# Retention and routed experts on one core: value products between the turns, casts and differences apart, decays by half, a head two products ahead

## The chip, the cores and the metric

The kernel runs on one core of a Trainium2 chip. Its time is the device time in microseconds, taken as the median of three runs. TensorE is called PE in the rows, VectorE DVE, ScalarE ACT, GpSimd POOL and SyncE SP.

## What is computed

Per batch and head a state of 64 x 64 decays and collects k v; each token's output is its query times the state. All 3072 tokens then go through a mixture of 8 experts: each token to the expert with the highest logit, weighted by that expert's probability and by a sigmoid.

```python
for t in range(S):                                   # B, H, S, D = 4, 8, 768, 64
    state = gamma * state + einsum('bhd,bhe->bhde', k[:, :, t], v[:, :, t])
    y[:, :, t] = scale * einsum('bhd,bhde->bhe', q[:, :, t], state)
x = y.transpose(0, 2, 1, 3).reshape(B * S, H * D)    # 3072 x 512
e_idx = argmax(x @ w_gate); probs = softmax(x @ w_gate); eom = sigmoid(x @ w_output_gate)
for e in range(8):                                   # w1[e]: 512 x 1024, w2[e]: 1024 x 512
    out[mask_e] = probs[mask_e, e] * eom[mask_e, e] * (relu(x[mask_e] @ w1[e]) @ w2[e])
```

## The kernel before

It has three parts. **Attention and routing** run over 12 pairs of chunks of 128 tokens (three pairs a batch). For a pair j, `load_pair` (L216) brings k, q and v on SyncE's queue, two pairs ahead; `prep_q` and `prep_v` (L255, L249) copy q and multiply v with its decays on GpSimd; `turn_k` and `turn_q` (L282, L291) transpose on TensorE, and ScalarE copies the results out of PSUM. `scores` (L302) multiplies keys and queries, and VectorE masks the result into `am` (L310). `inter` (L315) adds the part carried in the state, `attend(j, c)` (L325) the masked scores times v, one call for each chunk c; `weigh(j, c)` (L332) multiplies with the query decays on VectorE, and `state(j, c)` (L338) updates the state. Routing of pair j - 1 runs inside pair j: `logits`, `turn_l`, `route1`, `exps`, `tokens`, `counts`, `labels`, `places`, `gates`, `rows` (L350 to L462). `scatter(j, c)` (L472) writes the rows of a chunk, sorted by expert, to HBM with an indirect DMA of GpSimd. The order on every engine is the order of the calls (L594 to L750): nothing is rescheduled.

**The head** is the first 256 rows of the expert that has most tokens after pair 2 (`pick`). After pair 8 its count is checked (`late`, L678 and L679), all engines read that flag in pair 10 (L620), and the rows are loaded (`head_load`, L518) and prepared (`head_prep`, L527). Products run as a generator (`head_all`, L573), 192 steps of one product, advanced by `run_head(n)`: block f of the first layer (`head_stage1`, 12 products, a relu on ScalarE and the remainder of it on VectorE, L553 and L554), then block f - 1 of the second (`head_stage2`, 12 products). It fills TensorE while the last pair is routed.

**The expert loop** (L901) goes over the rest of that expert and the seven others in order of their counts, eight blocks each. Each float32 operand is split in a rounded part (a cast on ScalarE) and a difference (VectorE), and three products make one. `load_weights(s)` (L137) loads block s, and `split_weights(s)` (L148) makes both parts: two casts (L158, L159), two differences (L160, L161); `w_at` says which blocks are loaded in which pair. `load_x` (L760) loads an expert's sorted rows, `prep_x` (L777) transposes and splits them. `load_x(0)` waits for all scatters and for the `pad` of unused slots; the pads for the other experts (`new_pad`, L875) and the SyncE reads of the seven ranks (L712) come before it or around it.

Buffers matter where they make waits: two wide PSUM tiles `w` (each of scores, turns and tokens takes the next), one PSUM tile each for y0, y1, state and `misc`, three buffers `raw` (weights, the head's rows and at first the decays), two for v, three for k, one for the copied q.

Of the kernel before, what the change touches and what calls it, by code (L numbers as in the profile page):

```python
# [10 lines left out]
F32 = mybir.dt.float32  # L11
# [21 lines left out]
def retention_moe_kernel(  # L33
# [101 lines left out]
    raws, wts, rank_e = {}, {}, {}  # L135
# [12 lines left out]
    def split_weights(s: int):  # L148
# [11 lines left out]
        nc.vector.tensor_sub(lo[:, 0], raw[:, 0], hi[:, 0].bitcast(F32))  # L160
        nc.vector.tensor_sub(perm(lo), r2, perm(hi).bitcast(F32))  # L161
        wts[s] = (hi, lo)

# [26 lines left out]
    with tc.manual_schedule(engines=None), ExitStack() as actx:  # L190
# [25 lines left out]
        def load_pair(j):  # L216
            load2(kn, k, "kn", j, 3)
            load_q(j)
            load2(vn, v, "vn", j, 2)
# [6 lines left out]

        load2(kn, k, "kn", 0, 3)
        nc.gpsimd.memset(wg, 0.0)
        nc.scalar.dma_start(gv, dec_v)
        nc.scalar.dma_start(wg[:, 0, :, 0:E], w_gate.rearrange("(g p) e -> p g e", p=P))  # L230
        nc.scalar.dma_start(wg[:, 0, :, E:2 * E], w_ogate.rearrange("(g p) e -> p g e", p=P))
        load_q(0)
        load2(vn, v, "vn", 0, 2)
        nc.sync.dma_start(gqn[:, 0].rearrange("p g t -> p (g t)"), dec_q.unsqueeze(1).broadcast_to([2, D, NG * P]))
        nc.sync.dma_start(gc[:, 0].rearrange("p c g -> p (c g)"), dec_c.unsqueeze(1).broadcast_to([2, D, NC * NG]))
        load_pair(1)

        def swap_halves():
            for n, h in enumerate(half):
                nc.gpsimd.tensor_copy(wg[h, 1, :, 0:2 * E], wg[half[1 - n], 0, :, 0:2 * E])  # L240
            for n, h in enumerate(half):
                nc.gpsimd.tensor_copy(gc[h, 1], gc[half[1 - n], 0])
                nc.gpsimd.tensor_copy(gqn[h, 1], gqn[half[1 - n], 0])
# [5 lines left out]
        def prep_v(j, engine):  # L249
            c = 2 * (j % NJ)  # L250
            vs[j] = ap.tile([P, 2, H, D], F32, name="vs", tag="vs", bufs=2)
            engine.tensor_mul(vs[j].rearrange("p c h d -> p (c h) d"), vn.pop(j).rearrange("p c h d -> p (c h) d"),
                              gv[:, c:c + 2].rearrange("p c h -> p (c h)").unsqueeze(2).broadcast_to([P, 2 * H, D]))
# [10 lines left out]
        prep_v(0, nc.gpsimd)  # L264
# [4 lines left out]
        pw = ps_1.tile([P, 512], F32, name="pw", tag="y1")  # L269
# [20 lines left out]

        def turn_q(j, halved=False):  # L291
# [10 lines left out]
        def scores(j):  # L302
            for c in range(2):
                w = wide()
# [9 lines left out]

        def inter(j):  # L315
            rt["py"] = [ps_1.tile([P, 512], F32, name="py", tag=f"y{c}") for c in range(2)]
# [8 lines left out]
        def attend(j, c):  # L325
            py = rt["py"][c]
            for g in range(NG):
                for hh in range(2):
                    nc.tensor.matmul(py[half[hh ^ c], g * P:(g + 1) * P], vs[j][:, c, 2 * g + hh], ams[c][:, hh, g],
                                     start=(j % NJ == 0 and c == 0 and g == 0), stop=True, skip_group_check=True)  # L330

# [18 lines left out]
        def logits(j):  # L350
            misc = rt["misc"] = ps_1.tile([P, 512], F32, name="misc", tag="misc")
# [17 lines left out]
        def route1(j):  # L369
# [3 lines left out]
            m2b = m2.unsqueeze(2).broadcast_to([P, 2, E])  # L373
            key = sm.tile([P, 2, E], F32, name="key2", tag="key2")
# [7 lines left out]
            d16 = sm.tile([P, 2, E], F32, name="d16", tag="d16")  # L382
            nc.vector.tensor_tensor(out=d16, in0=lg[:, :, 0:E], in1=m2b, op=ALU.subtract)
# [25 lines left out]
        def counts(j):  # L409
# [11 lines left out]
            for c in range(2):  # L421
                nc.gpsimd.tensor_add(acc, acc, oh[:, c])
# [49 lines left out]
        def scatter(j, c):  # L472
# [4 lines left out]
            tc.declare_no_dep(st.ins, group="srt", reason="rows are disjoint")  # L477
            tc.add_to_no_dep_group("srt", st.ins)
            sent.append(st.ins)
# [18 lines left out]
        def sort8(c8, last, by):  # L498
# [15 lines left out]
        w_at = {4: (0,), 5: (1,), 6: (2,), 7: (3,), 8: (4,), 9: (5,), 10: (6, 7)}  # L514
# [3 lines left out]
        def head_load():  # L518
            t = wpool.tile([P, 8 * SEG], F32, name="xl0", tag="raw", bufs=3).rearrange("p (n x) -> p n x", x=SEG)
            for a in range(4):  # L520
# [3 lines left out]
                behind(ld, sent)  # L524
            hd["t"] = t

        def head_prep():  # L527
            t = hd["t"]
            hd["xh"] = hpool.tile([P, NDC, HEAD], F32R, name="xh0")
            hd["xl"] = hpool.tile([P, NDC, HEAD], F32R, name="xw0")  # L530
            for g in range(2):
# [5 lines left out]
                nc.vector.tensor_sub(hd["xl"][:, 2 * g:2 * g + 2], tp, hd["xh"][:, 2 * g:2 * g + 2].bitcast(F32))  # L537
            hd["idx"] = hpool.tile([P, HEAD // 32], I32, name="idx0")
            nc.vector.tensor_copy(hd["idx"], t[:, :, P])

        def head_stage1(f):
            hi, lo = wts[f]
            ps = ps_1.tile([P, 512], F32, name="h0", tag="st" if f == 0 else f"y{1 - f % 2}")[:, 0:HEAD]
            n = 0
            for r, ls in (("xh", (hi, lo)), ("xl", (hi,))):
                for dc in range(NDC):
                    for l in ls:
                        nc.tensor.matmul(ps, l[:, 0, dc * P:dc * P + P], hd[r][:, dc], start=(n == 0), stop=(n == 3 * NDC - 1))
                        n += 1
                        if n < 3 * NDC:  # L550
                            yield
# [41 lines left out]

        idle(9)  # L594
# [464 lines left out]
```

## Time and profile before

| | us |
|---|---|
| median of three runs (459.74 to 460.03) | 459.8 |
| the profiled execution | 461.23 |
| its span, first to last instruction | 459.5 |
| TensorE busy in the span | 422.1 |
| VectorE, ScalarE, GpSimd busy | 268.6, 177.8, 187.3 |

The profiled execution is 1.43 us above the median; 1.73 us of it lie outside its span. A busy TensorE need not be one at its best, since products are pipelined and their ends are modelled: the starts of neighbouring products tell the pace. Idle time is shown in brackets with what ended it.

### The profile page before, as it was taken

The page shows a single profiled execution, that of the slowest core. Times are in us where ns is not written, and L with a number is a line of the kernel's source. Part 1 is how long each engine was busy: PE and PEld are TensorE (multiplying, and loading weights), DVE is VectorE, ACT ScalarE, POOL GpSimd, SP SyncE. Part 2 cuts the span into 40 slices and gives each one's busy share as a digit, 9 for nine tenths or more (in the row PEclk, how much of TensorE's full clock was granted, in tenths as well). Part 3 has the DMA queues.
Part 4 walks back from the last instruction along what each step waited for, and adds up shares of the span by engine and source line. Part 5 has one row for each costly group of instructions (what it writes and reads, how often), then busy time and mean ns, then how long its engine had stood idle before and what let it go on. Part 6 is the DMA issues. An engine that isn't in the chain of part 4 may idle for free.

```text
span 459.5 us, 10306 instructions
## 1 busy us (share of the span) xinstructions
PE 422.1 (92%) x3701; PEld 401.6 (87%) x3701; DVE 268.6 (58%) x703; ACT 177.8 (39%) x392; POOL 187.3 (41%) x255
## 2 busy tenths in 40 slices
PE   8689999999696986999999999999999999999991
PEld 4579998888585986999999999999999999999990
DVE  2567777877866644684655656565565566565110
ACT  2034544555352511463443443444344353443111
POOL 5245666665611420643102442452452452441532
PEclk9979999999987997999999999999999999999997
DMA  8798689999631239469438448547547648630102
GB/s 151 178 233 195 173 227 264 278 272 268 191 84 35 95 83 228 152 219 247 132 106 196 149 142 184 169 143 181 167 162 166 185 157 184 199 121 14 36 18 69
DMA packets 126818, 74.15 MB, mean 161 GB/s; under 512 B 56854, under 2 KB 115098, under 8 KB 126756
## 3 DMA queue, kind: packets, MB, share of 16 engines
q1 hardware_dynamic: 119828, 59.57, 51.7%
q0 software_dynamic: 5728, 13.76, 8.4%
q8 instruction: 31, 0.51, 0.5%
q14 instruction: 31, 0.25, 0.2%
q10 hardware_dynamic: 1200, 0.06, 0.2%
HBM read 59.62 MB, written 15.23 MB: 163 GB/s over the span
## 4 chain that ended last, share of the span: by engine, by line
PE 51%; issue 7%; POOL 3%; DVE 1%; DMA 1%; ACT 0%; POOLq 0%; ACTq 0%
PE h L803 26%; PE a L821 24%; POOL out_dram L165 3%; DMA srt<-zrow,padr 1%; PE w L569 1%; DVE xt L789 0%; ACT xh L790 0%; DVE xw L791 0%; POOL srt L175 0%; POOLq L165 0%; ACT h L553 0%; POOLq L933 0%; DVE padr L738 0%; DVE ordf L730 0%; DVE ck L733 0%
## 5 line engine op out<-in xcount | busy, mean ns | idle before, releaser
L165 POOL DMA_INDIRECT out_dram<-ot,idi x83 | 86.9, 1047 | 151.2 <-ACT hh L807 123.8
L803 PE MATMUL h<-xh,whi 128*128 128x192 f32 (+7 forms) x256 | 86.6, 338 | 0.0
L803 PE MATMUL h<-xh,wlo 128*128 128x192 f32 (+7 forms) x256 | 86.5, 338 | 0.0
L803 PE MATMUL h<-xw,whi 128*128 128x192 f32 (+7 forms) x256 | 86.5, 338 | 0.0
L821 PE MATMUL a<-hl,whi 128*128 128x192 f32 (+7 forms) x256 | 85.7, 335 | 0.0
L821 PE MATMUL a<-hh,wlo 128*128 128x192 f32 (+7 forms) x256 | 85.7, 335 | 0.0
L821 PE MATMUL a<-hh,whi 128*128 128x192 f32 (+7 forms) x256 | 85.6, 335 | 0.0
L808 DVE SCALAR_TENSOR_TENSOR hl<-h,hh 128x192 fp32r<-128x192 f32 (+7 forms) x64 | 34.8, 544 | 66.9 <-ACT hh L807 66.7
L160 DVE TENSOR_TENSOR wlo<-raw,whi 128x512 fp32r<-128x512 f32 x64 | 44.2, 690 | 36.8 <-ACT whi L158 36.8
L807 ACT ACTIVATE hh<-h 128x192 fp32r<-128x192 f32 (+7 forms) x64 | 30.7, 480 | 88.8 <-PE h L803 88.8
L158 ACT CAST whi<-raw 128x512 fp32r<-128x512 f32 x64 | 39.8, 622 | 37.7 <-PE a L821 34.6
L803 PEld LDWEIGHTS h<-xh,whi 128*128 128x128 f32 x256 | 49.1, 192 | 0.5
L803 PEld LDWEIGHTS h<-xw,whi 128*128 128x128 f32 x256 | 49.0, 191 | 0.5
L803 PEld LDWEIGHTS h<-xh,wlo 128*128 128x128 f32 x256 | 48.9, 191 | 0.5
L821 PEld LDWEIGHTS a<-hl,whi 128*128 128x128 f32 x256 | 48.2, 188 | 0.6
L821 PEld LDWEIGHTS a<-hh,whi 128*128 128x128 f32 x256 | 48.2, 188 | 0.5
L821 PEld LDWEIGHTS a<-hh,wlo 128*128 128x128 f32 x256 | 48.3, 189 | 0.4
L161 DVE TENSOR_TENSOR wlo<-raw,whi 128x512 fp32r<-128x512 f32 x64 | 45.4, 709 | 0.0
L159 ACT CAST whi<-raw 128x512 fp32r<-128x512 f32 x64 | 39.7, 620 | 0.0
L474 POOL DMA_INDIRECT srt<-row,posi x24 | 24.6, 1026 | 17.8 <-ACT row L460 13.2
L790 ACT CAST xh<-xt 128x416 fp32r<-128x416 f32 (+3 forms) x32 | 16.3, 510 | 40.1 <-DVE xt L789 35.9
L310 DVE TENSOR_TENSOR am<-w,mask 128x1024 f32<-128x1024 f32 x24 | 28.3, 1215 | 5.5 <-PE w L307 5.5
(170 smaller groups left out, 633.3 us busy)
## 6 DMA issues: line engine op xcount, KB each, us to landing
raw<-in_moe_w_dram SPq DMA_DIRECT2D x128, 256.0 KB, 3.0
kn<-in_k_dram SPq DMA_DIRECT2D x24, 256.0 KB, 5.7
qn<-in_q_dram SPq DMA_DIRECT2D x12, 512.0 KB, 6.8
vn<-in_v_dram SPq DMA_DIRECT2D x24, 256.0 KB, 6.0
xl<-srt SPq DMA_DIRECT2D x12, 211.2 KB, 5.6
xl<-srt SPq DMA_DIRECT2D x12, 195.0 KB, 5.3
out_dram<-ot,idi POOLq DMA_INDIRECT x83, 2.6
xl<-srt SPq DMA_DIRECT2D x4, 227.5 KB, 6.5
```

The source lines that it names most:

```text
L158: nc.scalar.copy(hi[:, 0], raw[:, 0])
L159: nc.scalar.copy(perm(hi), r2)
L160: nc.vector.tensor_sub(lo[:, 0], raw[:, 0], hi[:, 0].bitcast(F32))
L161: nc.vector.tensor_sub(perm(lo), r2, perm(hi).bitcast(F32))
L165: st = nc.gpsimd.indirect_dma_start(out=dst, out_offset=bass.IndirectOffsetOnAxis(ap=idx, axis=0), in_=src, in_offset=None, bounds_check=n ...
L310: nc.vector.tensor_tensor(out=a.rearrange("p b g t -> p (b g) t"), in0=w.rearrange("p b (g t) -> p (b g) t", g=NG), in1=mask.rearrange("p ...
L474: st = nc.gpsimd.indirect_dma_start(out=srt, out_offset=bass.IndirectOffsetOnAxis(ap=posi[:, c:c + 1], axis=0), in_=row[:, c].rearrange("p ...
L790: nc.scalar.copy(xh[:, dc, w], tp[:, w])
L803: nc.tensor.matmul(ps[:, 0:C], l[:, 0, w], r[:, dc, 0:C], start=(n == 0), stop=(n == 3 * NDC - 1))
L807: relu = nc.scalar.activation(hh, ps[:, 0:C], AF.Relu)
L808: nc.vector.scalar_tensor_tensor(out=hl, in0=ps[:, 0:C], scalar=0.0, in1=hh.bitcast(F32), op0=ALU.max, op1=ALU.subtract)
L821: mm = nc.tensor.matmul(accs[d][:, 0:C], l[:, 1, w], r, start=(f == 0 and n == 0), stop=(f == NF - 1 and n == 2))
```

## The change

It rewrites the order of calls in pairs and tail, and some helpers. In the start, q is loaded first, k and v behind it; the decays of the queries come as two DMAs of 64 rows each in place of one DMA of [2, 64, 512], likewise the chunk decays; the gate weights are loaded later; `prep_v` of pairs 0 and 1 works in two halves; pair 0 is written out apart, with the state of pair 1 inside its scores. From pair 2 on k is loaded behind q and v. In a pair, GpSimd prepares the next q and v ahead of its first scatter; `attend(j, 0)` and `weigh(j, 0)` stand between the turns of k and q; the second scatter waits for that `attend`. `split_weights` becomes `cast_weights` (right behind the scores) and `low_weights` (behind the first weighing). Weights are loaded in pairs 4, 6, 8 and 9 only. The padding of the head's expert and the check of its count come in pairs 9 and 10. The head runs its first-layer blocks two ahead of the second layer, in three PSUM tiles. The SyncE reads of the seven ranks and the small operations behind them come after `load_x(0)`; nine operations that make the last flag come after the head.

```diff
@@ loads at the start
+        load_q(0)
         load2(kn, k, "kn", 0, 3)
+        load2(vn, v, "vn", 0, 2)
...
-        nc.sync.dma_start(gqn[:, 0].rearrange("p g t -> p (g t)"), dec_q.unsqueeze(1).broadcast_to([2, D, NG * P]))
+        for n, h in enumerate(half):
+            nc.sync.dma_start(gqn[h, 0].rearrange("p g t -> p (g t)"), dec_q[n:n + 1].broadcast_to([D, NG * P]))
@@ weights
+    def cast_weights(s: int):
...
         nc.scalar.copy(hi[:, 0], raw[:, 0])
         nc.scalar.copy(perm(hi), r2)
-        nc.vector.tensor_sub(lo[:, 0], raw[:, 0], hi[:, 0].bitcast(F32))
-        nc.vector.tensor_sub(perm(lo), r2, perm(hi).bitcast(F32))
         wts[s] = (hi, lo)
+        def rest():
+            nc.vector.tensor_sub(lo[:, 0], raw[:, 0], hi[:, 0].bitcast(F32))
+            nc.vector.tensor_sub(perm(lo), r2, perm(hi).bitcast(F32))
+        subs[s] = rest
@@ head
-            for f in range(1, NF):
+            yield from head_stage1(1)
+            for f in range(2, NF):
                 yield from head_stage1(f)
-                yield from head_stage2(f - 1)
+                yield from head_stage2(f - 2)
+            yield from head_stage2(NF - 2)
             yield from head_stage2(NF - 1)
@@ pairs, the new order
+        for j in range(1, NPR - 1):
             if j + 2 < NPR:
                 load_pair(j + 2)
...
+            prep_q(j + 1, nc.gpsimd)
+            prep_v(j + 1, nc.gpsimd)
+            if j >= 2 and j - 2 != EARLY:
+                scatter(j - 2, 0)
+            open_y()
+            scores(j, (lambda: state(1, 0)) if j == 1 else None)
+            if j - 1 in w_at:
+                cast_weights(w_at[j - 1])
             inter(j)
...
+            logits(j - 1)
+            turn_k(j + 1)
+            turn_l(j - 1)
+            route1(j - 1)
+            exps(j - 1)
+            done = attend(j, 0)
+            weigh(j, 0)
+            turn_q(j + 1)
+            gates(j - 1)
             if j >= 2 and j - 2 != EARLY:
-                scatter(j - 2, 1)
+                scatter(j - 2, 1, [done])
...
+            if j - 1 in w_at:
+                low_weights(w_at[j - 1])
             if j % NJ < NJ - 1:
                 state(j, 1)
+            tokens(j - 1)
+            labels(j - 1)
+            rows(j - 1)
+            counts(j - 1)
+            places(j - 1)
...
+            if j - 1 == EARLY:
+                judge()
             attend(j, 1)
             weigh(j, 1)
+            state(j + 1, 0)
@@ between head and loop
         load_x(0)
+        io_ = mp.tile([P, E], F32, name="io_", bufs=1)
...
+        for r in range(1, E):
+            rank_e[r] = nc.values_load(order[0:1, r - 1:r], engines=(mybir.EngineType.SP,), min_val=0, max_val=E - 1)
...
+        cast_weights(7)
+        low_weights(7)
         run_head(24)
         new_pad(hd["relu", 6])
+        run_head(12)
+        turn_x(0, 0)
+        turn_x(0, 1)
+        low_x(0, 0)
...
+        run_head(12)
+        new_pad(hd["relu", 7])
         run_head(1000)
```

## Rows read from the trace of the kernel before

**Rows 1.** From the page's second part: the clock granted to TensorE in 40 equal slices of the span, in tenths.

```profile
PEclk9979999999987997999999999999999999999997
```

**Rows 2.** Busy time of each engine by stage; columns: stretch and its length, busy time (instructions) of PE, PE's weight loads, DVE, ACT, POOL, granted clock, DMA share, GB/s. The cuts are the first score products of pairs 0, 1, 3, 4, 5, 6, 10, 11, then pair 11 and the head to the loop.

```profile
10.45:26.12 15.67, 9.73 (x144) 8.22 (x144) 9.02 (x12) 2.42 (x5) 5.99 (x8) 0.91 0.76 183
26.12:37.75 11.63, 11.45 (x174) 10.52 (x172) 6.30 (x28) 4.27 (x12) 4.02 (x8) 0.83 0.93 182
47.05:56.98 9.93, 9.75 (x163) 8.89 (x159) 6.86 (x30) 5.12 (x15) 6.38 (x11) 1.00 0.68 176
56.98:66.75 9.77, 9.59 (x177) 8.75 (x173) 7.66 (x35) 4.77 (x14) 6.00 (x10) 1.00 0.85 215
66.75:75.98 9.23, 9.10 (x159) 8.27 (x156) 6.15 (x28) 3.91 (x12) 5.59 (x10) 1.00 0.92 256
75.98:118.30 42.32, 39.12 (x647) 34.67 (x643) 33.05 (x119) 23.27 (x61) 27.69 (x41) 1.00 1.04 268
118.30:133.32 15.02, 11.05 (x176) 10.26 (x173) 11.20 (x33) 5.78 (x16) 5.95 (x10) 0.89 0.45 135
133.32:143.10 9.78, 5.43 (x93) 4.87 (x90) 6.73 (x12) 3.22 (x8) 1.03 (x1) 0.81 0.26 83
143.10:150.75 7.65, 6.63 (x62) 6.14 (x61) 4.40 (x26) 2.39 (x9) 2.65 (x7) 0.80 0.09 35
150.75:173.30 22.55, 21.04 (x188) 20.44 (x187) 12.38 (x67) 6.42 (x19) 7.43 (x12) 1.00 0.30 93
173.30:180.48 7.18, 3.06 (x14) 2.81 (x14) 2.90 (x9) 1.69 (x5) 0.98 (x1) 0.75 1.12 224
```

**Rows 3.** The timeline of the start: start and length in us, engine, line, operation, out<-in, shape, count, and in brackets the idle time before it with what ended it.

```profile
10.21 1.90 POOL L252 TENSOR_TENSOR vs<-vn,gv 128x1024 f32<-128x1024 f32 x1 [3.92 <-DMA vn<-in_v_dram]
...
18.95 0.66 PE L286 MATMUL w<-ident,kn 128*128 128x128 f32 x4 [1.21 <-DMA kn<-in_k_dram]
...
23.11 1.90 POOL L252 TENSOR_TENSOR vs<-vn,gv 128x1024 f32<-128x1024 f32 x1 [5.39 <-DMA vn<-in_v_dram]
...
25.07 1.12 PE L344 MATMUL st<-vs,kn 128*64 128x64 f32 x16 [2.52 <-POOL vs L252]
```

**Rows 4.** Stretches of the start, columns as in rows 2: ahead of, during and behind the load of the decays.

```profile
4.50:7.00 2.50, 2.50 (x13) 1.76 (x12) 0.00 (x0) 0.00 (x0) 1.53 (x15) 1.00 1.24 241
...
10.50:12.00 1.50, 1.50 (x24) 1.50 (x26) 0.15 (x1) 0.46 (x1) 1.50 (x1) 1.00 0.13 49
...
15.75:18.00 2.25, 2.00 (x38) 1.59 (x34) 1.40 (x2) 0.37 (x1) 1.93 (x4) 1.00 1.04 260
```

**Rows 5.** The timeline of pair 6, columns as in rows 3: the second weight difference and the turn of k.

```profile
78.48 1.09 DVE L161 TENSOR_TENSOR wlo<-raw,whi 128x512 fp32r<-128x512 f32 x1
...
80.76 1.09 PE L286 MATMUL w<-ident,kn 128*128 128x128 f32 x8 [0.95 <-DVE am L310]
```

**Rows 6.** The timeline where VectorE and GpSimd work side by side, in pair 0 and in pair 10, columns as in rows 3.

```profile
21.43 0.68 DVE L246 TENSOR_TENSOR gq<-gqn,gc 128x512 f32<-128x512 f32 x1
...
24.02 2.14 DVE L246 TENSOR_TENSOR gq<-gqn,gc 128x512 f32<-128x512 f32 x2
...
120.17 1.01 POOL L474 DMA_INDIRECT srt<-row,posi  x1 [0.30 <-ACT whi L159]
...
120.87 3.38 DVE L509 SCALAR_TENSOR_TENSOR cj<-cnts,first 128x8 f32<-128x8 f32 x1
121.18 1.17 POOL L259 COPY qr<-qn 128x512 f32<-128x512 f32 x2
122.31 1.90 POOL L252 TENSOR_TENSOR vs<-vn,gv 128x1024 f32<-128x1024 f32 x1
...
124.29 0.15 DVE L679 TENSOR_SCALAR late<-cnt 128x1 int32<-128x1 f32 x1
...
125.36 0.77 PE L355 MATMUL misc<-yt,wg 128*32 128x128 f32 x16 [3.97 <-DVE late L679]
```

**Rows 7.** The timeline from pair 11 to the loop, columns as in rows 3.

```profile
141.33 1.97 PE L450 MATMUL w<-ident,yt 128*128 128x128 f32 x8 [4.35 <-DVE am L310]
...
157.16 0.28 PE L548 MATMUL h<-xh,whi 128*128 128x256 f32 x1
157.28 0.28 PE L548 MATMUL h<-xh,wlo 128*128 128x256 f32 x1
...
163.07 0.47 PE L569 MATMUL w<-h,whi 128*128 128x256 f32 x2 [1.44 <-DVE h L554]
...
167.21 2.75 SPq L765 DMA_DIRECT2D xl<-srt  x3
...
173.10 0.17 DVE L784 CAST idi<-xl 128x6 int32<-128x6 f32 x1 [3.15 <-DMA srt<-zrow,padr]
...
177.51 1.04 PE L569 MATMUL w<-h,whi 128*128 128x256 f32 x2 [4.12 <-ACT h L553]
```

**Rows 8.** The chain that ended last, in order of time, at the loop's beginning: start, length, what, count.

```profile
180.68 4.19 PE h L803 x24
184.87 1.34 PE a L821 x12
```

**Rows 9.** The timeline of pair 2 behind the counts, columns as in rows 3.

```profile
45.38 0.23 POOL L468 TENSOR_SCALAR ef<-mk 128x2 f32<-128x2 f32 x1
...
45.39 0.16 DVE L440 SCALAR_TENSOR_TENSOR pos<-mk,rank 128x2 f32<-128x2 f32 x1
```

More of the change, by code (lines that the diff above doesn't have):

```diff
@@ L300, in turn_q, with scores @@
             qt[j] = o
-        def scores(j):
+        def scores(j, between=None):
             for c in range(2):
+                if c and between:
+                    between()
                 w = wide()
@@ L476, in scatter @@
                 in_=row[:, c].rearrange("p a x -> p (a x)"), in_offset=None, bounds_check=OV + NT - 1, oob_is_err=False)
-            tc.declare_no_dep(st.ins, group="srt", reason="rows are disjoint")
+            tc.declare_no_dep(st.ins, group="srt", keep=hd.get("pad", ()), reason="rows are disjoint")
             tc.add_to_no_dep_group("srt", st.ins)
+            behind(st, after)
+            if j > EARLY:
+                for ld in hd["loads"]:
+                    tc.declare_no_dep(st.ins, ld, reason="slots behind the rows loaded")
             sent.append(st.ins)
@@ L524, in head_load, with head_turn @@
                 behind(ld, sent)
+                hd["loads"].append(ld.ins)
             hd["t"] = t
-        def head_prep():
+            st = pad(pad0)
+            for ld in hd["loads"]:
+                tc.declare_no_dep(st.ins, ld, reason="slots behind the rows loaded")
+            hd["pad"] = [st.ins]
+            sent.append(st.ins)
+        def head_turn():
             t = hd["t"]
@@ L597, in retention_moe_kernel @@
         turn_q(0, True)
-        idle(3)
-        for j in range(NPR):
-            last = j + 1 == NPR
+        turn_k_parts(0)
+        load_gates()
+        load_pair(2)
+        open_y()
+        scores(0)
+        state(0, 0)
+        swap_halves()
+        more_gq(0, nc.vector)
+        attend(0, 0)
+        weigh(0, 0)
+        inter(0)
+        state(0, 1)
+        more_gq(1, nc.vector)
+        attend(0, 1)
+        weigh(0, 1)
+        idle(2)
+        prep_q(1, nc.vector)
+        turn_q(1, True)
@@ L677, in retention_moe_kernel @@
[L677 to L681 removed]
+            state(j + 1, 0)
+        load_weights(5)
+        j = NPR - 1
+        scatter(j - 2, 0)
+        scatter(j - 2, 1)
+        open_y()
+        scores(j)
+        inter(j)
+        logits(j - 1)
+        head_turn()
+        load_weights(6)
+        turn_l(j - 1)
+        route1(j - 1)
+        exps(j - 1)
@@ L704, in retention_moe_kernel @@
-        sent.append(pad(pad0).ins)
-        run_head(12)
-        for s in w_at[NPR - 2]:
-            split_weights(s)
-        io_ = sm.tile([P, E], F32, name="io_", tag="io_")
-        nc.vector.scalar_tensor_tensor(out=io_, in0=first, scalar=-float(16 * NT), in1=io8, op0=ALU.mult, op1=ALU.add)
-        top = sort8(cnts, io_, order)
-        for r in range(1, E):
-            rank_e[r] = nc.values_load(order[0:1, r - 1:r], engines=(mybir.EngineType.SP,), min_val=0, max_val=E - 1)
-        run_head(12)
+        run_head(6)
```

310 lines of the change are left out of this document (165 added, 145 removed).

## Prediction, before the changed kernel ran

> **What bounds the kernel now.** The profiled execution took 461.23 us, 1.4 above the median of 459.8, so I sum against 461.23 and give the result against the median. I read the clock first [rows 1]: it is below full in slices 3, 12, 13 and 16, so there are stops of TensorE, and all of them (but the end) lie in the first 40%. Then a table of stages, cut where TensorE begins the scores of each pair of chunks [rows 2]. From 180.5 us on the expert loop runs, which the change hardly touches. What can be gained lies ahead of it: 15.67 us for pair 0 with 9.73 busy, 11.63 us for pair 1 at clock 0.83, 42.32 us for pairs 6 to 9, 15.02 us for pair 10, and 47.16 us (9.78 + 7.65 + 22.55 + 7.18) from the scores of pair 11 to the first product of the expert loop. Pairs 3, 4 and 5 are the measure of an undisturbed pair: 9.93, 9.77 and 9.23 us (the three kinds differ in their state products), nearly all of it busy TensorE. The third view is the timeline around each gap [rows 3 to 8].
>
> **The start.** Pair 0 waits for loads. The third tile (v of pair 0) is there at 10.21 us, but pair 1's k and v only at 18.95 and 23.11, and the first state product of pair 1 runs at 25.07 [rows 3]. Between them the transfers collapse: while the query decays are under way the DMA share is 0.13 and 49 GB/s, against 241 ahead of it and 260 behind [rows 4]. 0.13 is two of sixteen engines, and the decay load is one DMA whose outermost dimension has two entries. By halves each DMA has 64 rows, so I let it run at some 230 GB/s (a little under the full stretches beside it): 0.26 MB is 1.1 us in place of about 5.5. Each tile of 0.52 MB is 2.3 us at that rate, so q1, k1, v1 land near 13.6, 15.8 and 18.1 us and q2, v2, k2 near 20.4, 22.7 and 25.0. If the halves gain nothing, pair 1's v stays near 23.
>
> The Trainium skill, DMA: Bandwidth & Descriptors, section Rules for kernel authors, speaks against the split: two transfers to disjoint partition halves serialize on the same engines, and one of 128 partitions is to be used. The same page, section Why a DMA increments its semaphore by 16 and not by 1, says that the number of engines divides the slowest dimension of both sides, which is two here; [rows 4] agree with that one. By the first rule alone the start would lose some 5 us of its gain; this is a rival below.
>
> With q first, pair 0 becomes a chain: v lands 10.2, half of its product with the decays is 0.95 (half of the 1.90 in [rows 3]), then the first state, attention, carried product, second state and attention, about 4 us of TensorE, weighing and the copy of q1 on VectorE 1.5, the turns of q1 and k1 2.1 and the last copies 0.8: scores of pair 1 start at about 19.4 in place of 26.12. That is **-6.7**. The state product that ran ahead of them moves behind them (+0.6), and the turn of k2 at 23.6 waits for its load until 25.0 (+1.4, bounds 0 and 3). Pair 1 becomes 9.77 + 2.0 = 11.8, at full clock, since no gap before it is longer than 1.5 us: **+0.2** against 11.63 at clock 0.83. Pairs 2 to 5 keep their work: **0**.
>
> **Pairs 6 to 9.** The turn of k waits on the masked scores of VectorE (0.95 us in pair 6), because the two weight differences lie ahead of them on that engine, the second one 1.09 us long [rows 5]. The change puts the casts ahead of ScalarE's other work and the differences after the first weighing, in the middle of the pair, and loads weights in four pairs only. Then each such pair costs what 3 to 5 cost: 9.93 + 9.77 + 9.23 + 9.93 = 38.86, **-3.5**. Moving half the value products between the turns of k and q adds no TensorE work; they need the first masked scores, which are some 2 us old by then. It gives VectorE a place for half the weighing early.
>
> **Pair 10.** VectorE needed 3.38 us for a product of eight columns while GpSimd ran its copies and its 1.90 us product, and all engines waited for that flag: TensorE 3.97 us, followed by a stretch at half clock (0.89 over the pair) [rows 6]. The flag is now made in pair 9, before the second weighing. What remains is the read of the flag and the branch: of the wait 0.9 lay behind the flag (124.44 to 125.36). 9.77 + 0.9 = 10.7: **-4.3**.
>
> **From pair 11 to the expert loop.** The head takes 192 products 0.12 us apart [rows 7], 23.0 us. The other 165 of the 357 TensorE records in these four stages, at pair 5's 9.23/159 = 0.058, are 9.6. So 32.6 us of work stand in 47.16. The gaps: 4.35 behind the masked scores, with the head's preparation ahead of them on VectorE; 1.44 for a delayed split of h; 4.12, the last, where the relu of block 7 queues on ScalarE behind casts that wait for rows landed at 173.10 [rows 7]; and half clock after each: the first 24 products of the loop take 4.19 in place of 2 x 1.34 [rows 8]. The change turns the head's rows without waiting for the differences, and with two blocks of first-layer products ahead a late relu is hidden by 24 products, 2.9 us. It also frees the rows of two delays: the early padding leaves the load's condition, and SyncE's reads of seven ranks, which came between, move behind the load (it was issued at 167.21). Each moved read still blocks SyncE, but behind it stand only the weights of block 8, not needed for eight blocks. I keep 2.2 us for what is new: the flipped logits of chunk 10 with no products to cover their copy (0.6), the first head block waiting for the first weighing and the differences of the rows (0.8), the branch (0.8). VectorE's 26.4 us of work (6.73 + 4.40 + 12.38 + 2.90) must fit in the shorter stretch and nearly fills what is left after pair 11's scores, so bounds are 33.5 and 38. 35.0: **-12.2**. In the loop 1.5 us of half clock go, while nine small operations of VectorE, moved there from ahead, hold the first h difference back by about 1: **-0.5**.
>
> Sum: -6.7 + 0.2 - 3.5 - 4.3 - 12.2 - 0.5 = **-27.0** with nothing taken back.
>
> **What the new order may add.** GpSimd now runs the copies of q and the product of v for the next pair before its scatter, so right behind its two additions to the running counts. VectorE's operation on rank and position starts then too: in pair 2 the additions end and the next GpSimd operation starts at 45.38, the position at 45.39 [rows 9]. That VectorE is held while GpSimd works on SBUF is seen twice: two products of decays, 0.68 each when alone, took 2.14 beside GpSimd's v product, and the 3.38 us above, which ended with GpSimd's last operation [rows 6]. Three small operations that can be held stand ahead of the second weighing, and the carried product of the next pair waits for it. Bounds for a pair: 0 if they slip through first; 1.35 if they wait until the v product ends (1.17 + 1.90, of which about 1.5 is free on the path); 1.6 where a weight difference has put them after the copies. I take the 1.6 for the four pairs with differences (5, 7, 9, 10), nearest to the 3.38 row because there the operations surely fall into GpSimd's work, and 0 for the others, where it is a matter of 0.01 us: **+6.4**.
>
> The Trainium skill, SBUF — State Buffer, section Who interferes with whom, has this as a rule: a VectorE instruction with two SBUF inputs contends with a GpSimd instruction that reads SBUF. The rows agree, though the 3.38 us spans three GpSimd instructions, not one. Were it one at a time, half of the 6.4 would go.
>
> Forecast: -27.0 + 6.4 = -20.6, 440.6 for a profiled execution, **439** for the median.
>
> **Rivals.** (a) The lock costs nothing: 459.8 - 27.0 = 433. For it: a pair has over a microsecond of room before the carried product. Against: [rows 6]. (b) Each of the ten pairs 1 to 10 is held, 10 x 1.35 to 1.6: 447. For it: the tie in [rows 9] recurs in each pair. (c) The halves of the decays gain nothing, v of pair 1 stays at 23: 5 us less, 444. Against: [rows 4]. (d) Slower: GpSimd's scatter follows the v product without a gap, and if VectorE is let in only when GpSimd stops, as in the 3.38 us, the hold grows by the scatter's 1.01 and its start [rows 6] to about 2.5, and with the differences 2.8 a pair; from 2.7 in all ten pairs it eats the whole 27, giving 461. Against: two weight differences did get in between copies, at 1.09 in place of 0.68 [rows 5].
>
> **How the numbers follow.** Forecast 0.41, (a) 0.27, (b) 0.18, (c) 0.10, (d) 0.04. The range takes (a) with 2 us of its bounds, the forecast, (c), and (b) with 2 us: 431 to 449. Faster by over 0.2% (0.9 us, about what a measurement of this kernel can tell from no change) is all but (d) and its neighbourhood: 0.95; same 0.01; slower 0.04.
>
> **What would show it.** Right: first scores of pair 1 near 19.4 us and no stretch at 49 GB/s; no wait of the turn of k on masked scores in pairs 6 to 9; TensorE never idle 4 us ahead of the loop; loop start near 160. The lock shows as position or rank operations far above 0.16 us and a wait of the carried product for the second weighing. Wrong if TensorE waits for VectorE throughout the head, or if loads of pair 2 hold pair 1 by more than 3 us.

## The result, and the profile after

The changed kernel took 445.12 us (median of four, 442.43 to 445.77) against 459.77: ratio 0.967, 95% interval [0.964, 0.971]. The forecast was 439, in a range of 431 to 449; the time lies in the range, 6.1 us above the forecast. The profiled execution is the fastest of the four, 442.43 us with a span of 440.7; the sum of the prediction for a profiled execution was 440.6.

Busy time by stage, cut at the first scores of pairs 1 to 11 and at the first product of the expert loop; columns as in [rows 2].

```profile
0.00:22.87 22.87, 18.24 (x155) 13.18 (x156) 10.30 (x17) 4.00 (x8) 11.76 (x43) 1.00 1.03 200
22.87:33.65 10.78, 10.78 (x189) 9.42 (x189) 7.61 (x28) 5.42 (x14) 4.66 (x9) 1.00 0.96 206
33.65:43.88 10.23, 9.61 (x160) 8.47 (x157) 8.99 (x29) 4.56 (x12) 5.82 (x10) 1.00 1.08 240
43.88:53.90 10.02, 10.02 (x164) 8.85 (x160) 7.27 (x29) 5.00 (x14) 6.79 (x12) 1.00 0.98 250
53.90:65.88 11.98, 10.38 (x176) 9.00 (x172) 9.90 (x35) 4.88 (x13) 5.84 (x11) 1.00 0.95 241
65.88:75.96 10.08, 9.62 (x160) 8.47 (x157) 8.81 (x21) 5.22 (x15) 5.60 (x8) 1.00 1.06 249
75.96:88.04 12.08, 10.02 (x161) 8.81 (x157) 9.89 (x38) 5.14 (x15) 7.05 (x14) 1.00 0.75 204
88.04:98.88 10.84, 10.38 (x177) 9.00 (x173) 9.50 (x29) 5.95 (x16) 6.28 (x10) 1.00 0.79 191
98.88:109.44 10.56, 9.62 (x161) 8.47 (x157) 9.15 (x29) 4.18 (x13) 6.01 (x12) 1.00 1.21 270
109.44:119.46 10.02, 10.02 (x164) 8.86 (x160) 8.08 (x31) 6.27 (x17) 6.23 (x10) 1.00 0.39 130
119.46:129.68 10.22, 10.11 (x176) 8.80 (x173) 8.41 (x27) 5.43 (x14) 7.00 (x9) 1.00 0.29 86
129.68:162.82 33.14, 32.56 (x350) 30.73 (x348) 26.03 (x111) 14.85 (x43) 11.20 (x20) 1.00 0.52 167
```

From pair 11 to the loop TensorE is now busy 32.56 of 33.14 us, and pair 10 is down from 15.02 to 10.22 [rows 2]. Pair 0 ends earlier, at 22.87 in place of 26.12. But pairs 2, 4, 5, 6, 7 and 8 each hold a gap that was not there: busy 9.61 of 10.23, 10.38 of 11.98, and so on. The waits of TensorE put one cause on all of them: line, what it waited for, sum in us, times, longest.

```profile
PE py L359 <- DVE yt L373: 6.1, 6, 2.1
```

That is the carried product waiting for the second weighing of the pair before. The timeline at the end of pair 3 shows why, columns as in [rows 3].

```profile
52.94 1.16 POOL L283 COPY qr<-qn 128x512 f32<-128x512 f32 x2
...
53.10 0.17 DVE L476 SCALAR_TENSOR_TENSOR junk<-misc,oh 128x8 f32<-128x8 f32 x1
...
53.19 0.38 DVE L479 SCALAR_TENSOR_TENSOR pos<-mk,rank 128x2 f32<-128x2 f32 x1
...
53.60 0.52 DVE L480 SCALAR_TENSOR_TENSOR rank<-rank,ov 128x2 f32<-128x2 f32 x1
...
54.06 1.90 POOL L275 TENSOR_TENSOR vs<-vn,gv 128x1024 f32<-128x1024 f32 x1
...
54.15 1.83 DVE L482 SCALAR_TENSOR_TENSOR posi<-pos,rank 128x2 int32<-128x2 f32 x1
...
57.10 0.68 DVE L373 TENSOR_TENSOR yt<-py,gq 128x512 f32<-128x512 f32 x1
```

Three operations on two columns take 0.38, 0.52 and 1.83 us. Each ends with one GpSimd instruction: the first copy, the second copy, the 1.90 us product. Between two of GpSimd's instructions VectorE gets one through. The weighing (57.10) stands behind them. The 3.38 us of [rows 6] do not fit this: that operation lasted past two copies and the product, and no run explains it. In the changed kernel, where no copy stands beside it, it takes 0.16 us (119.72).

The start of the changed kernel, columns as in [rows 3], and one stretch of it, columns as in [rows 2]:

```profile
10.59 3.68 PE L342 MATMUL w<-qt,kt 64*128 64x128 f32 x32
...
18.43 1.04 POOL L275 TENSOR_TENSOR vs<-vn,gv 128x512 f32<-128x512 f32 x1 [4.39 <-DMA vn<-in_v_dram]
...
22.87 1.16 PE L342 MATMUL w<-qt,kt 64*128 64x128 f32 x16 [0.88 <-DVE kt L301]
```

```profile
10.00:12.00 2.00, 2.00 (x16) 1.67 (x16) 0.69 (x1) 0.00 (x0) 1.14 (x2) 1.00 0.48 89
```

The product of pair 1's v with its decays starts at 18.43 in place of 23.11 [rows 3]. The slow transfers are shorter, not gone: 53 GB/s from 10.0 to 11.5 us, where the kernel before had 48 from 9.5 to 12.0 and 90 over the whole of 9.5 to 16.0. And 32 scores of pair 0 take 3.68 us; in the profiles where they start at full pace they take 2.06 (below).

### The profile page after: what moved, and what is told of

Read it like the earlier page. It is cut to its first block, busy times and chain, and to the rows that moved or that the text cites. A ratio compares the mean times of both kernels' runs of the same rounds, so it can differ in the third digit from the quotient of the medians.

```text
span 440.7 us, 10306 instructions
## 1 busy us (share of the span) xinstructions
PE 418.6 (95%) x3696; PEld 395.8 (90%) x3696; DVE 277.3 (63%) x701; ACT 179.3 (41%) x392; POOL 185.4 (42%) x255
## 4 chain that ended last, share of the span: by engine, by line
PE 51%; issue 7%; POOL 3%; POOLq 0%; DVE 0%
PE h L874 26%; PE a L892 26%; POOL out_dram L176 3%; POOLq L176 0%; POOLq L1045 0%; DVE hl L879 0%; DVE a L1012 0%
## 5 line engine op out<-in xcount | busy, mean ns | idle before, releaser
L874 PE MATMUL h<-xh,whi 128*128 128x192 f32 (+7 forms) x256 | 85.7, 335 | 0.0
L874 PE MATMUL h<-xh,wlo 128*128 128x192 f32 (+7 forms) x256 | 85.6, 334 | 0.0
L163 DVE TENSOR_TENSOR wlo<-raw,whi 128x512 fp32r<-128x512 f32 x64 | 43.8, 685 | 30.2 <-ACT whi L158 28.7
L874 PEld LDWEIGHTS h<-xh,whi 128*128 128x128 f32 x256 | 48.2, 188 | 0.4
L164 DVE TENSOR_TENSOR wlo<-raw,whi 128x512 fp32r<-128x512 f32 x64 | 43.7, 683 | 0.3 <-DVEq L807 0.3
```

The costliest lines, as they stand in the source:

```text
L874: nc.tensor.matmul(ps[:, 0:C], l[:, 0, w], r[:, dc, 0:C], start=(n == 0), stop=(n == 3 * NDC - 1))
```

## The experiments

Twelve runs were made, of ten kernels and on three chips; scatter_again and scatter_k_first_again repeat two kernels on the third chip. The kernel before took 459.5 us on the first (the first four runs), 466.0 on the second, 469.9 on the third, so ratios are compared, and stages of TensorE. In pairs 2 to 9 these are the same on all three: with the scatter first and nothing else changed there, 77.49 us in scatter_first, scatter_one_ahead and scatter_again, one on each chip.

| run | median us | ratio to before [95%] |
|---|---|---|
| same_again | 443.57 | 0.967 [0.964, 0.970] |
| late_places | 440.40 | 0.958 [0.956, 0.961] |
| scatter_first | 433.45 | 0.944 [0.941, 0.946] |
| fillers | 444.97 | 0.970 [0.968, 0.972] |
| whole_decays (second chip) | 454.29 | 0.973 [0.967, 0.978] |
| scatter_weights (second) | 443.52 | 0.951 [0.946, 0.956] |
| scatter_one_ahead (second) | 442.31 | 0.951 [0.945, 0.956] |
| scatter_k_first (second) | 440.78 | 0.944 [0.940, 0.949] |
| scatter_again (third) | 445.33 | 0.949 [0.944, 0.954] |
| scatter_values_late (third) | 439.89 | 0.939 [0.932, 0.945] |
| scatter_reads_early (third) | 445.19 | 0.951 [0.945, 0.956] |
| scatter_k_first_again (third) | 441.64 | 0.942 [0.935, 0.948] |

**The level.** 

> The changed kernel, unedited. It gives the level that the edits sent with it are held against, and a second profile. If the 2.7 us between its profiled execution (442.4) and its other executions (445.1 to 445.8) come from TensorE's granted clock in the start, the scores of pair 1 begin at 22.9 us when the time is 442.4 and near 25 us when it is 445; if they come from elsewhere, the start is the same in both profiles and another stage is longer.

The time is the changed kernel's (its profiled execution 442.08). Pairs 2 to 10 last the same within 0.01 us as in the first profile; the start moves. The rows are the scores of pairs 0 and 1.

```profile
10.60 3.24 PE L342 MATMUL w<-qt,kt 64*128 64x128 f32 x32
...
22.04 1.16 PE L342 MATMUL w<-qt,kt 64*128 64x128 f32 x16 [0.88 <-DVE kt L301]
```

The half pace ended somewhat earlier and pair 1 began 0.83 us earlier. Both profiled executions are the fastest of their runs, so the question in the expectation is not answered. The record gives TensorE's mean granted clock for each execution, and the time goes with it: 0.992 at 442.1 and 442.4 us, 0.985 to 0.989 in the others of both runs (443.3 to 446.4). By an estimate from these numbers, 0.006 of 443 us is 2.7 us. In which stage the clock was lower is not shown.

**The lock.** Two edits, one that moves VectorE's operations and one that moves GpSimd's.

```diff
-            places(j - 1)          # late_places: with choose(), judge() ...
             attend(j, 1)
             weigh(j, 1)
+            places(j - 1)          # ... behind the second weighing
```

> The three operations that give a token its place, and what follows them (choice and judgement of the first expert), are moved behind the second weighing of the pair. Theory: the waits of the carried product for the second weighing (6.1 us over pairs 1 to 8) come from these operations being held by GpSimd's copies ahead of the weighing; so the waits go, and the time falls by 5 to 6 us. Rival: the second weighing is late in itself (VectorE is full up to there), the waits stay and the time is that of the changed kernel within 1 us. Second rival: the held operations now delay the masked scores of the next pair instead, and 2 to 4 us stay.

```diff
+            if j >= 2 and j - 2 != EARLY:     # scatter_first
+                scatter(j - 2, 0)
             prep_q(j + 1, nc.gpsimd)
             prep_v(j + 1, nc.gpsimd)
-            if j >= 2 and j - 2 != EARLY:
-                scatter(j - 2, 0)
```

> GpSimd takes the first scatter of a pair ahead of its copies of q and its v product, so these can't start until the places are there. Theory of the lock: position, rank and integer position take 0.16 us each again in every pair, the waits of the carried product fall from 6.1 to under 1.5, the time falls by 4 to 6 us if GpSimd's later copies delay no turn of q. Rival: VectorE's small operations are slow for another cause (their PSUM operands, queueing), and keep 0.38, 0.52 and 1.83 us.

late_places won 3.2 us. The waits of the carried product are gone, and in their place the turn of k waits for the masked scores, which the held operations now delay: the second rival. The waits of TensorE:

```profile
PE w L310 <- DVE am L345: 4.1, 6, 1.2
```

In the timeline rank is now the operation that GpSimd's 1.90 us product holds; in the changed kernel it was the integer position:

```profile
44.91 1.83 DVE L480 SCALAR_TENSOR_TENSOR rank<-rank,ov 128x2 f32<-128x2 f32 x1
```

scatter_first won 10.1 us, more than expected. The scatter needs the places, so GpSimd's copies behind it can't meet them. The end of pair 3 in its timeline, and pairs 2 and 6 in the table of stages:

```profile
50.71 0.16 DVE L479 SCALAR_TENSOR_TENSOR pos<-mk,rank 128x2 f32<-128x2 f32 x1
...
50.90 0.16 DVE L480 SCALAR_TENSOR_TENSOR rank<-rank,ov 128x2 f32<-128x2 f32 x1
...
51.10 0.16 DVE L482 SCALAR_TENSOR_TENSOR posi<-pos,rank 128x2 int32<-128x2 f32 x1
...
52.05 1.03 POOL L513 DMA_INDIRECT srt<-row,posi  x1 [1.52 <-DVE base L656]
...
53.09 1.16 POOL L283 COPY qr<-qn 128x512 f32<-128x512 f32 x2
```

```profile
32.21:41.40 9.19, 9.19 (x160) 8.26 (x156) 6.85 (x28) 4.55 (x12) 6.57 (x10) 1.00 1.03 246
...
70.58:80.53 9.95, 9.95 (x161) 8.78 (x157) 8.14 (x40) 4.95 (x15) 6.47 (x13) 1.00 0.98 252
```

All three operations are at 0.16, and TensorE is never idle in pairs 2 to 9. Those pairs last 77.5 us (32.21 to 109.70) in place of 85.8 (33.65 to 119.46): **the lock cost 8.3 us** in the profile, 6.1 of them as the wait that the trace prints and 2.2 at its edges (pair 2: 1.04 us longer at a printed wait of 0.62). The profiled executions of same_again and of this version are 8.5 us apart (442.08 and 433.60): besides the 8.3, pair 2 began 0.9 us earlier (32.21 and 33.15), in a start that is the same program in both, and the loop took 0.9 longer. The other 1.6 of the 10.1 between the medians are not explained.

**The start.**

```diff
         turn_q(0, True)
+        idle(4)                    # fillers
         turn_k_parts(0)
+        idle(3)
```

> Four idle products behind the turn of q and three behind the turn of k of pair 0, as the kernel before had them. Theory: the half pace of TensorE from 6.2 to 14.2 us is what put the first scores of pair 1 at 22.9 in place of 19.4; with the fillers the pace is full from about 8 us, the scores begin 2 to 3 us earlier, and the time falls as much. Rival: the start waits for loads and copies all the same, the fillers only fill gaps, and the time is the same within 0.7 us.

The theory falls: the time was 1.4 us above same_again's (444.97 and 443.57, with intervals that overlap), not 2 to 3 below. The rival is near, though its 0.7 us is missed. TensorE was at full pace at once and pair 1 began at 20.39, 2.5 us earlier than in the changed kernel, and the gain was given back inside pair 1, which took 14.62 us (20.39 to 35.01) in place of 10.78. The rows are the scores of pair 0, the two waits of pair 1, and pair 1 as a stage:

```profile
10.01 2.06 PE L342 MATMUL w<-qt,kt 64*128 64x128 f32 x32
...
25.66 0.63 PE L310 MATMUL w<-ident,kn 128*128 128x128 f32 x4 [0.80 <-DMA kn<-in_k_dram]
...
27.52 0.66 PE L310 MATMUL w<-ident,kn 128*128 128x128 f32 x4 [1.23 <-DMA kn<-in_k_dram]
```

```profile
20.39:35.01 14.62, 12.59 (x189) 10.63 (x189) 7.88 (x28) 5.42 (x14) 6.65 (x13) 0.88 1.14 235
```

With TensorE early, pair 1 waits 2.03 us for the k of pair 2, and behind these waits the granted clock falls (0.88 over the pair, 0.76 from 28 to 35 us), which costs about the other 1.8 us (an estimate: 0.12 of 14.62). In the changed kernel pair 1 had no such wait and a clock of 1.00.

```diff
-        for n, h in enumerate(half):   # whole_decays: both decay loads in one DMA each
-            nc.sync.dma_start(gqn[h, 0]..., dec_q[n:n + 1].broadcast_to([D, NG * P]))
+        nc.sync.dma_start(gqn[:, 0]..., dec_q.unsqueeze(1).broadcast_to([2, D, NG * P]))
```

> The changed kernel with the query decays and the chunk decays loaded by one DMA each again, whose outermost dimension is two. Theory: the load by halves is what keeps the transfers near 200 GB/s; undone, a stretch of some 5 us at about 50 GB/s comes back ahead of pair 1's loads, the first scores of pair 1 begin near 25 to 27 us and the time rises by 4 to 5 us. Rival: two transfers to halves of the partitions run one behind the other on the same engines, the split gained nothing, and the time stays within 1 us.

The theory, in the stages: pair 1 began at 25.07 us and pair 2 at 37.60. In ten profiles with halves and the same order of loads pair 2 began between 32.2 and 35.8 us, in the two of them on this chip at 33.68 and 32.46, so 3.9 to 5.1 earlier. The ratio is 0.6% worse than the changed kernel's on another chip, some 2.7 us, with intervals that overlap. TensorE waits for the copy of q1, then goes on at half pace, and the slow transfers stand in two stretches:

```profile
10.00:12.00 2.00, 2.00 (x44) 1.84 (x43) 1.51 (x3) 0.00 (x0) 0.98 (x1) 1.00 0.28 60
...
14.00:16.00 2.00, 2.00 (x36) 1.41 (x34) 0.00 (x0) 0.37 (x1) 0.00 (x0) 1.00 0.53 108
```

```profile
20.49 2.00 PE L328 MATMUL w<-ident,qr 128*128 128x128 f32 x8 [4.42 <-DVE qr L281]
...
25.07 2.08 PE L340 MATMUL w<-qt,kt 64*128 64x128 f32 x16 [0.88 <-DVE kt L299]
```

```diff
-            if j < 2:                  # scatter_k_first, with the fillers
+            if j < 3:
                 load2(kn, k, "kn", j, 3)
                 load2(vn, v, "vn", j, 2)
```

> The version with the scatter first, and in it the fillers of the start, and k loaded ahead of v for pair 2. Theory: pair 1 ends when the k of pair 2 has landed and been turned (0.15 to 1.5 us of waits at 25.4 to 28.4 us in three traces), so the fillers alone moved nothing; with k ahead of v the wait goes, pair 2 begins 1.5 to 2.5 us earlier and the time is about 431 to 432. Rival: all loads of the start are bound by their bytes, and v of pair 2 is then late by as much for the state product: same time within 0.7 us.

> The version with the scatter first, with the fillers of the start and k ahead of v for pair 2, beside its own base. In its first profile pair 3 began at 40.8 us and the base's at 41.4, so 0.3 to 1.5 us faster than scatter_again are expected; rival: the landing of the start's loads varies by more than that from execution to execution, and the two are the same within 0.7 us.

In both profiles the wait for k is gone and pair 2 begins at 31.16 and 31.18 us; in its own base on the third chip it began at 35.80, behind 3.4 us of that wait (the longer part is the row) and at a granted clock of 0.89 over pair 1. Pair 2 gives 0.5 to 0.6 back (9.66 and 9.83 in place of 9.19). Beside that base the median is 3.7 us lower (441.64 and 445.33), with intervals that overlap; over the chips the ratios are 0.944 and 0.942 against 0.944 and 0.949. The wait is shown; its worth in the median is not settled.

```profile
27.28 0.63 PE L310 MATMUL w<-ident,kn 128*128 128x128 f32 x4 [3.05 <-DMA kn<-in_k_dram]
```

**Weights, head, reads and value products**, each undone in the version with the scatter first.

```diff
-            if j - 1 in w_at:          # scatter_weights: ahead of inter(j)
-                cast_weights(w_at[j - 1])
...
             state(j + 1, 0)
+            if j - 1 in w_at:
+                split_weights(w_at[j - 1])
```

> The version with the scatter first, and in it casts and differences of the weights of four blocks together again, at the end of the pair, as the kernel before had them. Held against the version with the scatter first. Theory: the differences then stand ahead of the masked scores on VectorE, the turn of k waits some 0.9 us in each of the four pairs, 3.5 us in all. Rival: without the lock VectorE has room for them there, and the time is the same within 1 us.

Pairs 6 and 8, each behind a block of weights, grew by 0.86 and 0.64 us, where the turn of k waits for the masked scores. Pair 10, behind the third block, has no such wait (it is 0.64 longer than in scatter_k_first on that chip, with idle time that the trace does not name). Behind the fourth, from pair 11 to the loop, nothing is lost (34.62 and 34.53). So 1.5 us are shown, between theory and rival. The median does not measure it: it is 2.7 above that of scatter_k_first, but that version also has the fillers and k ahead of v, and began pair 2 2.5 us earlier (31.16 and 33.68); the unedited version did not run on that chip.

```profile
76.50 1.09 PE L310 MATMUL w<-ident,kn 128*128 128x128 f32 x8 [0.79 <-DVE am L345]
...
97.06 1.09 PE L310 MATMUL w<-ident,kn 128*128 128x128 f32 x8 [0.58 <-DVE am L345]
```

```diff
-            yield from head_stage1(1)  # scatter_one_ahead
-            for f in range(2, NF):
+            for f in range(1, NF):
                 yield from head_stage1(f)
-                yield from head_stage2(f - 2)
+                yield from head_stage2(f - 1)
```

> The version with the scatter first, and in it the head's second layer follows one block behind the first layer, as the kernel before had it, in place of two (three of the padding writes move by 12 products with it). Theory: a relu that is late on ScalarE or a late split on VectorE then shows as a wait of TensorE of 0.5 to 2 us at several of the eight blocks, 2 to 4 us in all. Rival: the waits of the kernel before came from casts and differences ahead of the relu, which stand elsewhere now; one block ahead is enough, and the time is the same within 1 us.

One block waited, not several: 1.64 us for the split of h, and the stretch from pair 11 to the loop took 36.24 us against 34.53 in scatter_k_first on that chip. Two blocks ahead are worth some 1.6 us here. It is the wait that shows it; the length of this stretch alone would not, since without this edit it lies between 33.1 and 36.8 us in the other runs with late reads.

```profile
145.11 0.39 PE L624 MATMUL w<-h,whi 128*128 128x256 f32 x1 [1.64 <-DVE h L609]
```

```diff
-        load_x(0)                      # scatter_reads_early
         top = sort8(cnts, io_, order, mp)
         for r in range(1, E):
             rank_e[r] = nc.values_load(...)
+        load_x(0)
```

> The version with the scatter first, and in it SyncE's reads of seven ranks, with the sort they need, stand ahead of the load of the expert's rows again. Theory: the load is issued 2 to 3 us later and its rows land later, the turned rows come late and the beginning of the expert loop is held by 1 to 3 us. Rival: the rows are there long before they are needed, the same within 0.7 us.

The load was issued 30.1 us after the first scores of pair 11 (121.85 to 151.91), in place of 26.4 in scatter_again (124.26 to 150.64) and 24.2 to 26.1 in the six other runs on these two chips: seven reads and the sort put it off by 3.7 to 5.9 us, not the 2 to 3 expected. TensorE waited 5.42 us at the end of the head, and the stretch took 41.15 us, against 36.84 in scatter_again and 34.2 and 35.0 in the two others on this chip. The rows: the two loads, of scatter_again and of this version, and the wait.

```profile
150.64 2.02 SPq L828 DMA_DIRECT2D xl<-srt  x4
```

```profile
151.91 2.00 SPq L828 DMA_DIRECT2D xl<-srt  x4
...
160.03 1.04 PE L624 MATMUL w<-h,whi 128*128 128x256 f32 x2 [5.42 <-ACT h L608]
```

Yet the medians are equal, 445.19 and 445.33. On this chip the base stops some 17 us into the loop, with TensorE, VectorE and ScalarE idle at once for a reason that the trace does not name ("issue", "remote"):

```profile
181.61 0.33 ACT L878 ACTIVATE hh<-h 128x192 fp32r<-128x192 f32 x1 [4.00 <-remote]
...
181.97 0.36 DVE L879 SCALAR_TENSOR_TENSOR hl<-h,hh 128x192 fp32r<-128x192 f32 x1 [3.56 <-issue]
...
181.99 0.36 PE L892 MATMUL a<-hh,whi 128*128 128x192 f32 x1 [3.59 <-issue]
```

Behind the stop the granted clock is 0.57 for 8 us. From the loop's first product to the end of the span the base took 285.1 us, the version with early reads 279.4: it lost 4.3 ahead of the loop and nothing to this stop. So in these two profiles what the late reads win is given back there. It is not the base alone: all seven profiles with late reads on the second and third chips have pauses of TensorE 16 to 25 us into the loop, partly put down to "issue", and loops of 283.6 to 286.4 us. On the first chip the five with late reads have none, and loops of 277.9 to 278.8. Early reads ran once, on the third chip, so whether it is they that avoid the stop is not shown.

```diff
-            done = attend(j, 0)        # scatter_values_late
-            weigh(j, 0)
             turn_q(j + 1)
...
+            attend(j, 0)
+            weigh(j, 0)
             attend(j, 1)
```

> The version with the scatter first, and in it the first half of the value products, with their weighing, moved back behind the places, next to the second half (the second scatter no longer waits for them). Theory of the prediction: moving them up added nothing and took nothing by itself, so the time is the same within 1 us. Rival: they cover the copy of the turned keys and give VectorE room ahead of the carried product; back in place, the turn of q or the carried product of the next pair waits 0.3 to 0.7 us in each of nine pairs, 3 to 6 us in all.

Neither: it was faster. Pairs 2 to 9 took 76.2 us in place of 77.5: 0.3 less in each of pairs 3, 4, 6, 7 and 9, nothing in 5 and 8, 0.1 more in 2. The timeline has no gap of TensorE in pair 3 of either; the rows are the value products of pair 3, with the products that follow them, in the version with the scatter first, in two stretches, and in this one, in one.

```profile
46.12 1.09 PE L366 MATMUL py<-am,vs 128*64 128x128 f32 x16
47.14 1.09 PE L330 MATMUL w<-ident,qr 128*128 128x128 f32 x8
...
49.94 1.09 PE L366 MATMUL py<-am,vs 128*64 128x128 f32 x16
50.86 0.63 PE L382 MATMUL st<-vs,kn 128*64 128x64 f32 x16
```

```profile
49.26 1.97 PE L366 MATMUL py<-am,vs 128*64 128x128 f32 x32
51.06 0.63 PE L382 MATMUL st<-vs,kn 128*64 128x64 f32 x16
```

By the starts, the 32 products take 1.80 us in one stretch (49.26 to 51.06), and 1.02 and 0.92 in two. The other 0.16 of the 0.3 us lie beside the first stretch: there the step from the turn of the logits to what follows it takes 0.10 longer and the turn of q 0.06. So in pair 3 the order with more breaks between kinds of products costs TensorE 0.3 us. In pair 5 the same places give 0.23 us, but the step from the turn of q to the next turn takes 1.16 us in place of 0.93 and takes it back; what holds it the trace does not name. The median is 5.4 us lower than scatter_again's, and the profiled spans 5.5: 1.3 in these pairs, 3.2 by an earlier end of pair 1 (32.61 in place of 35.80), where the load of k varies, 2.7 from pair 11 to the loop, where the base ran at a granted clock of 0.84 for the first 10.7 us, less 1.7 elsewhere. Only the 1.3 can be put down to the edit. This is the lowest ratio of all, 0.939, with an interval that overlaps those of scatter_first and scatter_k_first.

## Why the prediction was right, and where it was off

The direction and the range held because most terms were read from the right gaps. That the sum came so near is partly luck: errors of +9.0 and -7.2 us cancel. Against the sum for a profiled execution, stage by stage (the lock stands in the stage whose carried product waits, one behind the pair whose operations are held):

| stage | forecast | measured | off |
|---|---|---|---|
| up to the scores of pair 1 | 19.4 | 22.87 | +3.5 |
| pair 1 | 11.8 | 10.78 | -1.0 |
| pairs 2 to 5 | 38.2 | 42.31 | +4.1 |
| pairs 6 to 9 | 38.9 + 3.2 | 43.50 | +1.4 |
| pair 10 | 10.7 + 1.6 | 10.22 | -2.1 |
| pair 11 to the loop | 35.0 + 1.6 | 33.14 | -3.5 |
| loop and end | 280.2 | 279.6 | -0.6 |

(The loop took 461.23 - 180.48 = 280.75 before, less 0.5.) The sum of the last column is +1.8, which is 442.4 against 440.6. The other 4.3 of the 6.1 lie between profile and median: I took the median 1.4 below the profiled execution as in the kernel before (1.6 as rounded), and it was 2.7 above. That step was not worked out from anything. The slower executions had a lower mean granted clock (0.985 to 0.989 against 0.992); why stays open, and the start, which varies from execution to execution (pair 2 began between 32.2 and 35.8 us in ten profiles), is a candidate only.

Of the signs named ahead, these came: no wait of the turn of k on masked scores in pairs 6 to 9, no idle 4 us ahead of the loop, and both signs of the lock. The scores of pair 1 at 19.4 did not come (22.87), 1.5 us at 53 GB/s were left of the stretch at 49, and the loop started at 162.82, not near 160. In the changed kernel the loads of pair 2 did not hold pair 1; in scatter_again they did, by 3.4 us.

**The lock** was the right mechanism, of the wrong size and in the wrong pairs. The forecast took 1.6 us for the operations of pairs 5, 7, 9 and 10, which have weight differences, and nothing for the others, because the tie in [rows 9] was "a matter of 0.01 us". It came from the operations of pairs 1 and 3 to 7, weights or not, 0.9 to 2.1 us each, as waits in pairs 2 and 4 to 8: 8.3 in all instead of 6.4. In pairs 2 and 8 the operations were a turn or two ahead of GpSimd and took 0.15 to 0.52 us, with no wait behind them, as the lower bound had it. In pairs 9 and 10, two of the four that the forecast charged, they took 0.16: GpSimd has the scatters first behind pair 9, and no copies at all behind pair 10. The order of calls shows both, and the forecast passed over it. The forecast's condition "were it one at a time" holds for these operations: VectorE and GpSimd take turns, one instruction each. The kernel before showed it already beside [rows 5]: while the two weight differences ran (0.74 us, then the 1.09 shown), GpSimd's two copies took 2.01 us in place of 1.17. The 3.38 us, on which the forecast leaned most, are the exception. That the cost would then be half does not follow, since the third of the three operations meets the longest instruction, the 1.90 us product. Rival (d) needed VectorE to be shut out until GpSimd stops, and fell by the same rows; (b), all ten pairs held, named too many. Its lower price for a pair does not come out of its own terms: 1.17 + 1.90 less 1.5 is 1.57, not 1.35.

The Trainium skill, SBUF — State Buffer, section Who interferes with whom, says that a VectorE instruction with at most one SBUF input, outside its 2-port modes, does not contend with GpSimd. The rows agree: the reduction with one of its two inputs in PSUM (53.10, 0.17 us) runs beside the copy, the next one with both inputs in SBUF is held.

**The start** was mis-sized by a step the prediction passed over: it priced TensorE's chain at full pace. Without the fillers of the kernel before the engine ran at half of it up to 14 us in the changed kernel's profile, and pair 1 began at 22.87 us. At the start of pair 2 the loss was 2.5 us (33.65 against 19.4 + 11.8 = 31.2). Full pace alone does not win it, as fillers shows: pair 2's k, for which the forecast gave 25.0 us with bounds of 0 and 3 on the wait, was turned between 25.1 and 28.4 where TensorE came early. With full pace and k ahead of v, pair 2 began at 31.16 and 31.18. The forecast also took pair 1 to be at full clock because no gap before it was longer than 1.5 us. It was at full clock, but that reason does not hold: in fillers two waits of 0.80 and 1.23 us were followed by 0.88, in scatter_weights two of 1.46 and 1.44 by 1.00. The split of the decays did what was forecast (pair 1's v at 18.43, forecast 18.1), and rival (c) falls: undoing it put pair 2 off by 3.9 to 5.1 us. The Trainium skill's rule against halves (DMA: Bandwidth & Descriptors, section Rules for kernel authors), which the forecast set against the split, is not the one that bears on it: another row of that section says that an outermost dimension of fewer than 16 confines a DMA to at most that many engines. The stretch at 49 GB/s with two of sixteen engines' share [rows 4] and the 60 and 108 GB/s above agree with that row.

**Pairs 6 to 9** without the lock take 39.1 us, against 38.9 forecast. **Pair 10** came within 0.5. **From pair 11 on** 2.2 us had been kept for new waits; only one of 0.39 was seen ahead of the loop (the same wait is 1.6 to 1.8 in six of the runs on the other chips). Late reads (5.4 us of wait if undone) and two blocks ahead (1.6) are both part of the 14 us that this stretch gave. **The value products**, costed at nothing, cost 1.3 us over pairs 2 to 9.

## What to carry to other kernels

Before moving GpSimd work, list what VectorE runs at that time with both inputs in SBUF and what waits for it: a 0.16 us operation can take as long as GpSimd's longest instruction. Give GpSimd's work a dependency that puts it behind those operations (here a scatter that needs their result), rather than moving VectorE's side, which only hands the wait on. When a stage is sped up, ask at once which load ends it next; and interleaving equal products with others is not free on TensorE (0.3 us a pair in five of eight pairs here).

## What the runs showed of the hardware beyond that

The granted clock is printed as 1.00 for the stretch from 10 to 12 us of the changed kernel, while 32 scores took 3.68 us in place of 2.06: in the first 14 us the pace of equal products tells more than that column. The version with the scatter first began its scores at the same place of the same program as the unedited kernel (10.35 and 10.59 us) and had full pace there, so this differs between executions: of the ten profiles without the fillers, three have half pace there (3.24 to 3.68 us) and seven full pace, from 9.4 to 10.4 us on. And chips differ: 459.5, 466.0 and 469.9 us for one kernel, with pauses in the loop on the second and third that the trace does not explain.
